# Separate banks for m and y, a shared ring for u and the transposes, u's products before the values', and the decayed keys on GpSimd

## The chip, the cores and the metric

The kernel runs on one core of one Trainium2 chip. The metric is the device time of one execution in microseconds. Five engines work side by side, each through its own queue in order: TensorE (PE, with its weight loads PEld), VectorE (DVE), ScalarE (ACT), GpSimd (POOL) and SyncE (SP, which here issues DMAs). Operands lie in SBUF; matmuls write to PSUM, which has 8 banks of 2 KB per partition.

## The reference

A linear attention with a decayed state feeds two expert layers. The change touches the attention alone.

```python
# B, H, S, D = 4, 8, 768, 48
for t in range(S):
    kt, vt, rt = (k[:, :, t], v[:, :, t], r[:, :, t])
    cur = np.einsum('bhd,bhe->bhde', u[None] * kt, vt)
    y[:, :, t] = np.einsum('bhd,bhde->bhe', rt, state + cur)
    state = w[None, :, :, None] * state + np.einsum('bhd,bhe->bhde', kt, vt)
# x = y as 3072 tokens x 384
expert_idx = np.argmax(xn @ en.T / tau, axis=1)      # xn, en: rows scaled to length 1
for e in range(8):                                   # one expert per token
    h = np.maximum(x[mask] @ w1[e], 0.0)
    out[mask] = gate_w[mask, None] * (h @ w2[e])
h = out @ w_in                                       # second layer, all tokens
y = (h * np.clip(h + 3.0, 0.0, 6.0) / 6.0) @ w_out
```

## The kernel before

The sequence is cut into 6 chunks of 128 tokens and the 8 heads into 4 pairs, so the attention has 24 groups (chunk c, head pair hp), each with all 4 batches. Within a chunk the recurrence becomes matmuls. For each group `load` (L556) brings four tiles from HBM through SP's queue: rk_t (r and k by dimension), tk (k by token), vd and vt (v by dimension and by token). rk_t and tk have three buffers, vd and vt five.

`scaled` (L656) multiplies r and k with powers of the decay: k_s (L659) and r_s (L660) on VectorE, rk_p (r times k, L662) on GpSimd, and kk, the keys by token times ktab (L666), on VectorE. kk is not made in the last chunk. `scores` (L669) makes the products of k_s and r_s on TensorE (L676); ScalarE copies them out (a_m, L679), and GpSimd sets the upper part to zero with two affine selects (L680). `current` (L685) makes m on TensorE (L691) from rk_p and the bonus u, and VectorE multiplies it with vd into mv (L693).

`outputs` (L696) makes y on TensorE: from the second chunk on the state's products (L704), then the values' products with the scores (L710), both into y_all; then u_ps (L717), the products of kk and vt for the next state. VectorE adds mv to y (y_sb, L719) and updates the state from u_ps (L724; in the first chunk ScalarE copies it, L722). `by_token` (L727) transposes y_sb on TensorE (L732) into x_ps, and ScalarE copies it into x_t (L735).

m and y are two halves of one tile, `my` of the pool psY (L653): for each of its two banks o, m has one half and y the other. u_ps has a bank of its own (psU), x_ps too (psX); psA holds two banks of scores, and psM has two buffers, which the routing's tiles (lt_ps, l_ps, rc_ps, li_ps), the tables' and the gathered rows' transposes (tp) take in turn. Together these are the 8 banks.

The loop over the groups (L765) does, for group i: the loads of group i+4; scores and m of group i+1; the transposes of group i-1; `scaled` for group i+2; in the first three groups of a chunk a step of the routing of the chunk before (`route`, L233); and the outputs of group i. TensorE's instructions keep this order (`pin`); on the other engines a planner orders them by their place in the program and by when it expects them to be ready. The routing sums a token's products with the expert directions, takes the best expert, its rank and weight, with some 20 short VectorE instructions per chunk (L253 to L303). It ends with the DMA that writes x_t to HBM (L306). x_t has two buffers; a memset on GpSimd (L758) opens each new one. From group 16 on, the first expert's weights are split on ScalarE and VectorE (`prep_w`, L203 and L206), and rows of the first expert are gathered and transposed. After the attention come the experts, and then the second layer.

Of the kernel before, what the change touches and what calls it, by code (L numbers as in the profile page):

```python
# [8 lines left out]
F32 = mybir.dt.float32  # L9
# [6 lines left out]
ALU = mybir.AluOpType  # L16
AX = mybir.AxisListType
ET = mybir.EngineType
PSUM = bass.MemoryType.PSUM
DRAM = bass.MemoryType.DRAM  # L20

B, H, S, D = 4, 8, 768, 48
# [4 lines left out]
C = 128  # L27
NCH = S // C
# [17 lines left out]
def rwkv_moe_kernel(ctx, tc, dT, tokA, wuT, uw, emb, tau, w1, w2, win, wout, out):  # L46
    nc = tc.nc
# [8 lines left out]
    psM = pctx.enter_context(tc.tile_pool(name="psM", bufs=2, space=PSUM))  # L56
# [56 lines left out]
    start = const.tile([128, E], F32, name="start")  # L113
# [429 lines left out]
    with actx:  # L543
# [6 lines left out]
        pa = ExitStack()  # L550
        psA = pa.enter_context(tc.tile_pool(name="psA", bufs=2, space=PSUM))
        psY = pa.enter_context(tc.tile_pool(name="psY", bufs=1, space=PSUM))
        psU = pa.enter_context(tc.tile_pool(name="psU", bufs=1, space=PSUM))
        psX = pa.enter_context(tc.tile_pool(name="psX", bufs=1, space=PSUM))

        def load(c, hp):  # L556
            rk_t = ld.tile([112, 2, B, C], F32, name="rk_t", tag="rk", bufs=3)
# [28 lines left out]
        ktab = st_p.tile([128, HP, 96], F32, name="ktab")  # L586
# [7 lines left out]
        n = 1  # L594
        while n < C:
            nc.vector.tensor_tensor(out=ptab[:, :, n + 1:2 * n + 1], in0=ptab[:, :, 1:n + 1],
                                    in1=ptab[:, :, n:n + 1].to_broadcast([112, HP, n]), op=ALU.mult)
# [52 lines left out]

        pin = tc.keep_in_program_order
        halves = ((0, 64), (64, 48))
        my = psY.tile([112, 2, 2, 2, C], F32, name="my")  # L653
        m_all, y_all = my[:, :, 0], my[:, :, 1]

        def scaled(c, hp, rk_t, tk, vd, vt):  # L656
            r_s = rk.tile([112, B, C], F32, name="r_s", tag="r", bufs=3)
            k_s = rk.tile([112, B, C], F32, name="k_s", tag="k")
            loads["k_s"] = nc.vector.tensor_tensor(out=k_s, in0=rk_t[:, 1], in1=itab[:, hp:hp + 1, :].to_broadcast([112, B, C]), op=ALU.mult).ins  # L659
            nc.vector.tensor_tensor(out=r_s, in0=rk_t[:, 0], in1=ptab[:, hp:hp + 1, 0:C].to_broadcast([112, B, C]), op=ALU.mult)  # L660
            rk_p = rk.tile([112, B, C], F32, name="rk_p", tag="ku")
            nc.gpsimd.tensor_tensor(out=rk_p, in0=rk_t[:, 0], in1=rk_t[:, 1], op=ALU.mult)  # L662
            kk = None
            if c < NCH - 1:
                kk = rk.tile([128, B, 96], F32, name="kk", tag="kk", bufs=3)
                nc.vector.tensor_tensor(out=kk, in0=tk, in1=ktab[:, hp:hp + 1, :].to_broadcast([128, B, 96]), op=ALU.mult)  # L666
            return r_s, k_s, rk_p, kk

        def scores(r_s, k_s):  # L669
# [14 lines left out]

        def current(c, hp, vd, rk_p):  # L685

            for o in range(2):
                for h in range(2):
                    q0, n = halves[(h + o) % 2]
                    r0 = 64 * h  # L690
                    pin(nc.tensor.matmul(m_all[q0:q0 + n, o], lhsT=ub[r0:r0 + 48, hp, 0:n], rhs=rk_p[r0:r0 + 48, 2 * o:2 * o + 2], start=True, stop=True))  # L691
            mv = rk.tile([112, B, C], F32, name="mv", tag="mv")
            nc.vector.tensor_tensor(out=mv.rearrange("p (o i) t -> p o i t", o=2), in0=m_all, in1=vd.rearrange("p (o i) t -> p o i t", o=2), op=ALU.mult)  # L693
            return mv

        def outputs(c, hp, vt, r_s, a_sb, kk, mv):  # L696
            s_n, s_o = (state[hp][(c - i) % 2] for i in range(2))
            if c > 0:
                for i in range(2):
                    for o in range(2):  # L700
                        for h in range(2):
                            q0, n = halves[(h + o) % 2]
                            r0, b = 64 * h, 2 * o + i
                            pin(nc.tensor.matmul(y_all[q0:q0 + n, o, i, :], lhsT=s_o[r0:r0 + 48, b, 0:n], rhs=r_s[r0:r0 + 48, b, :],  # L704
                                                 start=(i == 0), stop=False, skip_group_check=True))
            for o in range(2):
                for i in range(2):
                    for q, (q0, n) in enumerate(halves):
                        b = 2 * o + i
                        pin(nc.tensor.matmul(y_all[q0:q0 + n, o, i, :], lhsT=vt[:, b, q0:q0 + n], rhs=a_sb[(q + o) % 2][:, b, :],  # L710
                                             start=(c == 0), stop=True, skip_group_check=True))
            if c < NCH - 1:
                u_ps = psU.tile([112, B, D], F32, name="u_ps", tag="u")
                for b in range(B):
                    for h, (p0, n) in enumerate(halves):
                        v0 = 64 * ((h + b // 2) % 2)
                        pin(nc.tensor.matmul(u_ps[p0:p0 + n, b, :], lhsT=kk[:, b, 48 * h:48 * h + n], rhs=vt[:, b, v0:v0 + 48], start=True, stop=True))  # L717
            y_s = yp.tile([112, B, C], F32, name="y_sb", tag="y")
            loads["y_s"] = nc.vector.tensor_tensor(out=y_s.rearrange("p (o i) t -> p o i t", o=2), in0=y_all, in1=mv.rearrange("p (o i) t -> p o i t", o=2), op=ALU.add).ins  # L719
            if c < NCH - 1:  # L720
                if c == 0:
                    nc.scalar.copy(s_n[:, :, 0:D], u_ps)  # L722
                else:
                    nc.vector.scalar_tensor_tensor(out=s_n[:, :, 0:D], in0=s_o[:, :, 0:D], scalar=ptab[:, hp, C:C + 1], in1=u_ps, op0=ALU.mult, op1=ALU.add)  # L724
            return y_s

        def by_token(c, hp, x_t, y_s):  # L727

            x_ps = psX.tile([128, 2, 4, 64], F32, name="x_ps", tag="x")
            for b in range(B):  # L730
                o, i = divmod(b, 2)
                pin(nc.tensor.transpose(x_ps[:, i].rearrange("p s d -> p (s d)")[:, o * 128:o * 128 + 112], y_s[:, b, :], ident[0:112, 0:112]))  # L732
            for h, slots in enumerate((slice(0, 4, 3), slice(1, 3))):
                d0 = hp * 96 + h * D
                loads["x_t"] = nc.scalar.copy(out=x_t[:, :, d0:d0 + D].rearrange("p (o i) d -> p i o d", o=2), in_=x_ps[:, :, slots, 0:D]).ins  # L735
# [4 lines left out]
        def prepare(i):  # L740
            if i < len(groups):
                if i < HP:
                    tables(i)
                pre[i] = scaled(*groups[i], *data[i])

        def begin(i):
            if i < len(groups):
                r_s, k_s, rk_p, kk = pre[i]
                a_sbs[i] = scores(r_s, k_s)
                mvs[i] = current(*groups[i], data[i][2], rk_p)  # L750

        def moved(i):

            if i >= 0:
                c, hp = groups[i]
                if hp == 0:
                    xs[c] = xp.tile([128, B, DG], F32, name="x_t", tag="x", bufs=2)
                    nc.gpsimd.memset(xs[c][:, :, DM + 1:DG], 0.0)  # L758
                by_token(c, hp, xs[c], ys[i])
# [5 lines left out]
        for i, (c, hp) in enumerate(groups):  # L765
# [7 lines left out]
            if pend and hp < 3:  # L773
                rest += step(pend, 1) or []
            r_s, _, _, kk = pre.pop(i)
            ys[i] = outputs(c, hp, data[i][3], r_s, a_sbs.pop(i), kk, mvs.pop(i))
            if pend and hp == 3:
                step(pend, 1)
# [71 lines left out]
    with ExitStack() as mctx:  # L850
# [78 lines left out]
        for e in range(E):  # L929
# [35 lines left out]
            n = CAPS[e] if e else NL  # L965
# [322 lines left out]
```

## Time and profile before

| | us |
|---|---|
| median of 3 runs | 827.93 |
| lowest, highest | 824.88, 828.96 |
| the profiled execution | 831.06 |
| its span | 829.4 |

The profile shows one execution. Its times are microseconds from the start of the span unless marked ns. Lines such as L710 are lines of the kernel. The granted clock of TensorE is given as a share of full speed, where 1.00 is 2.4 GHz and 0.50 is 1.2 GHz. In a timeline, instructions of one line that follow each other are merged (x16); the idle time of the engine ahead of them and what ended it stand in brackets. Whom a wait is put down to is inferred from semaphores, and a wait for several of them is put down to the last.

| engine | busy us | share of the span |
|---|---|---|
| PE | 780.8 | 94% |
| DVE | 505.0 | 61% |
| ACT | 333.9 | 40% |
| POOL | 196.3 | 24% |

### The profile page before, as it was taken

The page shows a single profiled execution, that of the slowest core. Times are in us where ns is not written, and L with a number is a line of the kernel's source. Part 1 is how long each engine was busy: PE and PEld are TensorE (multiplying, and loading weights), DVE is VectorE, ACT ScalarE, POOL GpSimd, SP SyncE. Part 2 cuts the span into 40 slices and gives each one's busy share as a digit, 9 for nine tenths or more (in the row PEclk, how much of TensorE's full clock was granted, in tenths as well). Part 3 has the DMA queues.
Part 4 walks back from the last instruction along what each step waited for, and adds up shares of the span by engine and source line. Part 5 has one row for each costly group of instructions (what it writes and reads, how often), then busy time and mean ns, then how long its engine had stood idle before and what let it go on. Part 6 is the DMA issues. An engine that isn't in the chain of part 4 may idle for free. (4 is left out here: it accounts for less than half of the span.)

```text
span 829.4 us, 13926 instructions
## 1 busy us (share of the span) xinstructions
PE 780.8 (94%) x5353; PEld 698.8 (84%) x5354; DVE 505.0 (61%) x1031; ACT 333.9 (40%) x669; POOL 196.3 (24%) x222
## 2 busy tenths in 40 slices
PE   6879877899999999999989999999999999999995
PEld 3767655578999999998979898999998998999995
DVE  8585888864767778778468888453333343333331
ACT  3333424634455455546343434343333333333331
POOL 6543533613442242222202111210002002001001
PEclk8896998989999999999999999999999999999998
DMA  9865768315664666553312222010001001001001
GB/s 259 239 196 158 230 208 256 117 40 181 215 206 153 202 201 191 191 190 115 111 32 73 58 57 58 31 46 1 0 1 39 1 1 38 1 1 39 1 1 38
DMA packets 32235, 86.56 MB, mean 104 GB/s; under 512 B 4348, under 2 KB 15681, under 8 KB 32160
## 3 DMA queue, kind: packets, MB, share of 16 engines
q1 hardware_dynamic: 28480, 75.58, 29.6%
q0 software_dynamic: 3680, 10.01, 3.5%
q8 instruction: 44, 0.72, 0.4%
q14 instruction: 31, 0.25, 0.1%
HBM read 72.94 MB, written 12.63 MB: 103 GB/s over the span
## 5 line engine op out<-in xcount | busy, mean ns | idle before, releaser
L422 PE MATMUL l<-xh,whi 128*128 128x512 f32 (+9 forms) x504 | 184.5, 371 | 2.7 <-DVEq L1134 2.7
L423 PE MATMUL l<-xl,whi 128*128 128x512 f32 (+9 forms) x504 | 186.9, 372 | 0.0
L424 PE MATMUL l<-xh,wlo 128*128 128x512 f32 (+9 forms) x504 | 185.8, 369 | 0.0
L458 DVE SCALAR_TENSOR_TENSOR rg<-rg,l 128x512 f32<-128x512 f32 x96 | 65.7, 687 | 134.2 <-ACT rg L457 133.6
L457 ACT ACTIVATE rg<-l,nums 128x512 f32<-128x512 f32 x96 | 65.9, 689 | 172.8 <-PE l L424 160.3
L473 PE MATMUL o<-wlo,hh 128*128 128x384 f32 x384 | 128.9, 336 | 0.0
L472 PE MATMUL o<-whi,hh 128*128 128x384 f32 x384 | 128.1, 336 | 0.0
L474 PE MATMUL o<-whi,hl 128*128 128x384 f32 x384 | 124.4, 336 | 0.0
L422 PEld LDWEIGHTS l<-xh,whi 128*128 128x128 f32 x504 | 95.2, 190 | 13.8 <-issue 3.9
L424 PEld LDWEIGHTS l<-xh,wlo 128*128 128x128 f32 x504 | 95.7, 190 | 12.8
L423 PEld LDWEIGHTS l<-xl,whi 128*128 128x128 f32 x504 | 95.7, 190 | 10.1
L460 DVE TENSOR_TENSOR hl<-rg,hh 128x512 fp32r<-128x512 f32 x96 | 66.7, 696 | 48.6 <-ACT hh L459 45.2
L459 ACT CAST hh<-rg 128x512 fp32r<-128x512 f32 x96 | 59.4, 621 | 64.8 <-DVE rg L458 52.5
L1196 POOL DMA_INDIRECT out_dram<-o_t,ctok x20 | 20.8, 1040 | 255.4 <-ACT o_t L1194 252.1
L472 PEld LDWEIGHTS o<-whi,hh 128*128 128x128 f32 x384 | 72.4, 189 | 4.1
L473 PEld LDWEIGHTS o<-wlo,hh 128*128 128x128 f32 x384 | 72.5, 189 | 3.5
L523 DVE SCALAR_TENSOR_TENSOR hl<-l,hh 128x192 fp32r<-128x192 f32 (+8 forms) x72 | 37.5, 534 | 58.6 <-ACT hh L522 58.6
L474 PEld LDWEIGHTS o<-whi,hl 128*128 128x128 f32 x384 | 72.1, 189 | 0.2
L423 PE MATMUL acc<-hl,whi 128*128 128x192 f32 (+8 forms) x216 | 72.0, 335 | 0.2 <-DVE hl L523 0.2
L424 PE MATMUL acc<-hh,wlo 128*128 128x192 f32 (+8 forms) x216 | 72.1, 335 | 0.0
L522 ACT ACTIVATE hh<-l 128x192 fp32r<-128x192 f32 (+8 forms) x72 | 33.1, 474 | 85.3 <-PE l L424 79.9
L422 PE MATMUL acc<-hh,whi 128*128 128x192 f32 (+8 forms) x216 | 65.1, 335 | 0.6 <-DVE x L973 0.6
(221 smaller groups left out, 1151.4 us busy)
## 6 DMA issues: line engine op xcount, KB each, us to landing
wst<-in_w_dram SPq DMA_DIRECT2D x32, 768.0 KB
rk_t<-in_dT_dram SPq DMA_DIRECT2D x24, 448.0 KB
vd<-in_dT_dram SPq DMA_DIRECT2D x24, 224.0 KB
vt<-in_tok_dram SPq DMA_DIRECT2D x24, 224.0 KB
xs_d<-x_t SPq DMA_DIRECT2D x6, 776.0 KB
tk<-in_tok_dram SPq DMA_DIRECT2D x24, 192.0 KB
q<-in_win_dram SPq DMA_DIRECT2D x12, 384.0 KB
q<-in_wout_dram SPq DMA_DIRECT2D x12, 384.0 KB
```

The source lines that it names most:

```text
L422: pin(nc.tensor.matmul(ps, lhsT=w[0], rhs=x[0], start=first, stop=False))
L423: pin(nc.tensor.matmul(ps, lhsT=w[0], rhs=x[1], start=False, stop=False))
L424: pin(nc.tensor.matmul(ps, lhsT=w[1], rhs=x[0], start=False, stop=last))
L457: nc.scalar.activation(out=r6, in_=ps, func=AF.Relu, bias=three)
L458: nc.vector.scalar_tensor_tensor(out=gf, in0=r6, scalar=6.0, in1=ps, op0=ALU.min, op1=ALU.mult)
L459: nc.scalar.copy(out=gh, in_=gf)
L460: nc.vector.tensor_tensor(out=gl, in0=gf, in1=gh.bitcast(F32), op=ALU.subtract)
L472: pin(nc.tensor.matmul(acc[t], lhsT=gh[:, sl], rhs=wh[:, f % 4, :], start=(f == span[0]), stop=False))
L473: pin(nc.tensor.matmul(acc[t], lhsT=gh[:, sl], rhs=wl[:, f % 4, :], start=False, stop=False))
L474: pin(nc.tensor.matmul(acc[t], lhsT=gl[:, sl], rhs=wh[:, f % 4, :], start=False, stop=(f == span[1] - 1)))
L522: last["a"] = nc.scalar.activation(out=hh[:, 0:n], in_=ps[:, 0:n], func=AF.Relu).ins
L523: last["v"] = nc.vector.scalar_tensor_tensor(out=hl[:, 0:n], in0=ps[:, 0:n], scalar=0.0, in1=hh[:, 0:n].bitcast(F32), op0=ALU.max, op1=ALU ...
```

## The change

m and y get tiles of their own, each with two banks of which half is used; u_ps and x_ps no longer have pools of their own but take turns with the routing's tiles in psM, which keeps its two buffers. On TensorE u's products now stand between the state's products and the values'. kk is computed on GpSimd. Nothing else differs.

```diff
-        psU = pa.enter_context(tc.tile_pool(name="psU", bufs=1, space=PSUM))
-        psX = pa.enter_context(tc.tile_pool(name="psX", bufs=1, space=PSUM))
...
-        my = psY.tile([112, 2, 2, 2, C], F32, name="my")
-        m_all, y_all = my[:, :, 0], my[:, :, 1]
...
-                nc.vector.tensor_tensor(out=kk, in0=tk, in1=ktab[:, hp:hp + 1, :].to_broadcast([128, B, 96]), op=ALU.mult)
+                nc.gpsimd.tensor_tensor(out=kk, in0=tk, in1=ktab[:, hp:hp + 1, :].to_broadcast([128, B, 96]), op=ALU.mult)
...
         def current(c, hp, vd, rk_p):
 
+            m_all = psY.tile([112, 2, 4, C], F32, name="m_ps", tag="m")[:, :, 0:2]
...
         def outputs(c, hp, vt, r_s, a_sb, kk, mv):
             s_n, s_o = (state[hp][(c - i) % 2] for i in range(2))
+            y_all = psY.tile([112, 2, 4, C], F32, name="y_ps", tag="y")[:, :, 0:2]
...
+            if c < NCH - 1:
+                u_ps = psM.tile([112, B, D], F32, name="u_ps", tag="m")
+                for b in range(B):
+                    for h, (p0, n) in enumerate(halves):
+                        v0 = 64 * ((h + b // 2) % 2)
+                        pin(nc.tensor.matmul(u_ps[p0:p0 + n, b, :], lhsT=kk[:, b, 48 * h:48 * h + n], rhs=vt[:, b, v0:v0 + 48], start=True, stop=True))
             for o in range(2):
                 for i in range(2):
                     for q, (q0, n) in enumerate(halves):
                         b = 2 * o + i
                         pin(nc.tensor.matmul(y_all[q0:q0 + n, o, i, :], lhsT=vt[:, b, q0:q0 + n], rhs=a_sb[(q + o) % 2][:, b, :],
                                              start=(c == 0), stop=True, skip_group_check=True))
-            if c < NCH - 1:
-                u_ps = psU.tile([112, B, D], F32, name="u_ps", tag="u")
-                for b in range(B):
-                    for h, (p0, n) in enumerate(halves):
-                        v0 = 64 * ((h + b // 2) % 2)
-                        pin(nc.tensor.matmul(u_ps[p0:p0 + n, b, :], lhsT=kk[:, b, 48 * h:48 * h + n], rhs=vt[:, b, v0:v0 + 48], start=True, stop=True))
...
-            x_ps = psX.tile([128, 2, 4, 64], F32, name="x_ps", tag="x")
+            x_ps = psM.tile([128, 2, 4, 64], F32, name="x_ps", tag="m")
```

## Rows read from the trace of the kernel before

**Rows 1.** Windows: stretch, length, then busy us by engine, PE clock, DMA share, GB/s

```profile
60.00:70.00 10.00, 7.48 (x80) 5.94 (x79) 6.02 (x8) 1.78 (x6) 3.54 (x5) 0.61 0.72 201
70.00:80.00 10.00, 10.00 (x126) 7.06 (x124) 4.93 (x10) 5.32 (x16) 5.09 (x7) 0.70 0.40 115
...
200.00:250.00 50.00, 50.00 (x300) 46.63 (x299) 34.42 (x67) 26.37 (x54) 17.85 (x15) 1.00 0.59 194
```

**Rows 2.** Waits, 20 to 185 us: who for whom, us in total, times, longest

```profile
PE my L704 <- DVE mv L693: 14.1, 10, 4.3
...
PE my L691 <- DVE y_sb L719: 9.2, 6, 2.1
...
PE x_ps L732 <- DVE y_sb L719: 2.2, 2, 1.6
```

**Rows 3.** Timeline of PE: start us, us, line, operation, tiles, count, wait before

```profile
62.98 1.13 PE L704 MATMUL my<-r_s,state 48*64 48x128 f32 x16 [2.52 <-DVE mv L693]
...
84.28 0.66 PE L691 MATMUL my<-rk_p,ub 48*64 48x256 f32 x8 [2.00 <-DVE y_sb L719]
...
86.18 1.13 PE L704 MATMUL my<-r_s,state 48*64 48x128 f32 x16 [0.52 <-DVE mv L693]
...
100.08 1.16 PE L676 MATMUL a_ps<-r_s,k_s 48*128 48x128 f32 x16
...
104.81 1.16 PE L676 MATMUL a_ps<-r_s,k_s 48*128 48x128 f32 x16
...
118.30 0.67 PE L704 MATMUL my<-r_s,state 48*64 48x128 f32 x16 [2.37 <-DVE mv L693]
...
132.88 1.13 PE L704 MATMUL my<-r_s,state 48*64 48x128 f32 x16 [4.28 <-DVE mv L693]
...
138.66 0.60 PE L732 MATMUL x_ps<-ident,y_sb 112*128 112x112 f32 x4
...
145.97 0.67 PE L704 MATMUL my<-r_s,state 48*64 48x128 f32 x16 [1.44 <-DVE mv L693]
146.57 1.09 PE L710 MATMUL my<-a_m,vt 128*64 128x128 f32 x16
```

**Rows 4.** Timeline of DVE

```profile
59.41 2.91 DVE L659 TENSOR_TENSOR k_s<-rk_t,itab 112x512 f32<-112x512 f32 x1 [0.54 <-PE a_ps L676]
62.25 0.68 DVE L693 TENSOR_TENSOR mv<-my,vd 112x512 f32<-112x512 f32 x1
...
79.71 1.10 DVE L257 TENSOR_TENSOR lg<-lg,mx 128x32 f32<-128x32 f32 x1
...
83.48 0.66 DVE L719 TENSOR_TENSOR y_sb<-my,mv 112x512 f32<-112x512 f32 x1
...
128.26 3.96 DVE L659 TENSOR_TENSOR k_s<-rk_t,itab 112x512 f32<-112x512 f32 x1
...
136.15 0.66 DVE L719 TENSOR_TENSOR y_sb<-my,mv 112x512 f32<-112x512 f32 x1
```

**Rows 5.** Timeline of POOL

```profile
60.57 1.21 POOL L680 TENSOR_SCALAR_AFFINE_SELECT a_m<-a_m 128x512 f32<-128x512 f32 x2
61.76 1.70 POOL L662 TENSOR_TENSOR rk_p<-rk_t 112x512 f32<-112x512 f32 x1
...
79.49 1.27 POOL L662 TENSOR_TENSOR rk_p<-rk_t 112x512 f32<-112x512 f32 x1
89.40 0.11 POOL L758 MEMSET x_t<- 128x12 f32 x1 [8.64 <-DMA xs_d<-x_t]
...
144.91 1.49 POOL L680 TENSOR_SCALAR_AFFINE_SELECT a_m<-a_m 128x512 f32<-128x512 f32 x2
```

**Rows 6.** Single lines: ns min/median/max; for L666 the groups' busy us and mean ns

```profile
L659 DVE TENSOR_TENSOR k_s<-rk_t,itab x20: 676/692/3959, 25.2 to 150.6; 112x512 f32<-112x512 f32 x20
L693 DVE TENSOR_TENSOR mv<-my,vd x22: 673/683/693, 26.4 to 162.6; 112x512 f32<-112x512 f32 x22
L662 POOL TENSOR_TENSOR rk_p<-rk_t x21: 1251/1272/1811, 21.8 to 153.3; 112x512 f32<-112x512 f32 x21
...
L666 DVE TENSOR_TENSOR kk<-tk,ktab 128x384 f32<-128x384 f32 x20 | 12.6, 632 | 0.3 <-PE u_ps L717 0.2
```

## The prediction

> **What bounds the kernel now.** I read the windows first: they say which engine sets the pace of which part. From 200 to 250 us TensorE is busy in all of 50.00 us at clock 1.00 [rows 1], and the change touches nothing from there on. From 20 to 172 us, the attention with its 24 groups, it is different: in 60 to 70 us TensorE works 7.48 of 10 us, and at clock 0.61 [rows 1]. So the change is worth what it does to that stage, and what the stage gains reaches the end whole, because the experts' matmuls follow it on the same engine and wait for little else.
>
> The waits of that stage name the places [rows 2]. TensorE's y products wait for VectorE's mv (L704, 14.1 us in 10 waits), its m products for y_sb (L691, 9.2 us in 6), its transposes for y_sb (L732, 2.2 us in 2). The first two are waits for a shared bank: my keeps m and y of one half in one bank, so y may not be written while mv reads m, nor m while y_sb reads y. TensorE's order of time shows the single waits [rows 3], VectorE's and GpSimd's why they are long [rows 4, 5]. There are two kinds.
>
> In the first, k_s stands in front of mv on VectorE and doesn't get through. At 59.41 it took 2.91 us, where its median is 0.69; GpSimd ran one instruction after the other, and k_s ended 0.54 us after the affine selects did (62.32 against 61.78), while the rk_p behind them took 1.70, where its median is 1.27 [rows 4 to 6]. At 128.26 it took 3.96. So an instruction of VectorE with both inputs in SBUF waits for GpSimd, past several instructions. mv and y_sb, with one input in PSUM, don't: mv's longest is 693 ns [rows 6].
>
> In the second kind the routing's short instructions stand in front of y_sb. At 79.71 the subtraction L257, on 32 columns only, took 1.10, again to the end of a rk_p on GpSimd (79.49+1.27); y_sb began at 83.48 only, and m waited 2.00 [rows 3 to 5].
>
> **The change part by part.** All is against the profiled run's own 831.06 us (span 829.4); the median of the three runs, 827.93, lies 3.13 lower.
>
> Own banks, first kind. The waits of y for mv at 62.98, 118.30 and 132.88 are 2.52+2.37+4.28 = 9.17 [rows 3]. With y in its own banks TensorE goes on with y, u, values and the next scores. What is late next is m of the next group, which may not overwrite m before mv has read it, and the transposes, which need y_sb. At 132.88 the worst case is that k_s still ends at 132.22: then y_sb still ends at 136.8 (136.15 and its 0.66), and the transposes behind it start there and not at 138.66 [rows 3, 4]; gain 1.8 of 4.28. At the two others I take off one kk, 1.0, that lengthens GpSimd's run: 1.5+1.4. Together **-4.7** (0 to -9.2).
>
> Own banks, second kind. Three times a chunk's routing makes m wait about 2.0, and y behind it another 0.52 (one of the three at 84.28 and 86.18) [rows 3]. The 0.52 goes. The first wait moves to the transposes, which stand behind m; TensorE gains the 0.6 that m takes (0.66, less some overlap). But kk now follows rk_p on GpSimd and holds up the routing's two-input instructions: +1.0. Three times (-0.52-0.6+1.0) = **-0.4**. The three other waits of m (9.2 less 6.1) lose 0.6 each: **-1.8**.
>
> The rest of y's waits, 14.1-9.17-1.56 = 3.4, goes too, except at 145.97: the values behind it start at 146.57, and their affine select ended at 146.40 (144.91+1.49) [rows 3, 5]. Of its 1.44 only 0.2 is won: **-2.1**.
>
> The clock. After the wait at 62.98 it was 0.61 and then 0.70 in the windows to 80 us [rows 1], so 3.9+3.0 = 6.9 us at full clock were not granted, most of it under work. That fall goes only if the wait before it goes; I take half, **-2.5** (0 to -6.9). The falls behind the routing stay, since their waits stay about as long.
>
> kk on GpSimd. VectorE loses 20 instructions of 632 ns, 12.6 us [rows 6]. GpSimd has no such shape; its rk_p on 112x512 takes 1.25 to 1.27, so kk on 128x384 lies between 0.95 (by columns) and 1.27; 1.0, as it is the same operation with fewer columns. Five of the 20 are counted above. For the other 15: behind the values stand scores and m, about 1.7, before the transposes need y_sb, which takes 0.69, so a delay of 1.0 is just covered in the steady groups; it isn't where GpSimd catches up. That happens once a chunk: the memset of x_t held its queue for 8.64 us before 89.40 [rows 5], and affine, rk_p and now kk of two groups follow it without a break. I take 0.2 each, **+3.0** (0 to +15). On GpSimd's queue the affine selects stand behind kk; kk waits for u's products of three groups earlier, and those come before the scores that the next selects work on, so it holds none up for long. Also tk comes free on GpSimd now, and SP's loads queue behind it; kk is needed three groups later, so nothing.
>
> The Trainium skill, SBUF — State Buffer, section "Who interferes with whom", has a rule for this: a VectorE instruction with two SBUF inputs and a GpSimd instruction that reads SBUF exclude each other, and the second waits until the first has finished. The trace agrees that they exclude each other, but the 2.91 and 3.96 are longer than any GpSimd instruction beside them [rows 4, 5], so here one waits past several. By the rule alone the two long runs would not grow by kk, and the sum would be 2.0 better.
>
> Ring of two. u and x_ps share psM with the routing's four tiles. Without a routing tile between them each gets its own old slot back; with one they change places, and the transposes then wait for the state update that reads u, right behind the y_sb for which they wait anyway. The trace of before doesn't show these waits: 0 to +2, the width of a few y_sb and state updates on VectorE, because in one group the gathered rows' transposes come straight behind u; **+0.5**. u before the values gives the affine select 0.6 us more, and takes it from y_sb's lead over the next scores; both were counted.
>
> Sum: -4.7-0.4-1.8-2.1-2.5+3.0+0.5 = -8.0. Profiled 823.1; as a median **820**.
>
> **The rivals.** *A, the lock decides (slower).* GpSimd's run per group becomes 1.21+1.27+1.0 = 3.5 us, and VectorE's k_s and r_s, of one shape, need 1.4 between them: 4.9, more than the 4.73 us of a group without a wait (scores at 100.08 and 104.81) [rows 3, 5, 6]. From there every kk is on the path. In the sum, take out the 3.0 and the five of 1.0 and put in 20 of 1.0 to 1.27: -16.0+20 = +4 to +9, a median of 832 to 837. For it: VectorE is already late wherever TensorE waits. Against: VectorE gets 12.6 us back, and GpSimd idled 8.64 us in one go [rows 5], so its work isn't the limit, only its place. The Trainium skill, GPSIMD Engine Reference, section 4.1, speaks for A: two-input elementwise work belongs on VectorE, being about twice as slow on GpSimd. The trace agrees on the size: rk_p takes 1.27, k_s 0.69 on the same shape [rows 6].
>
> *B, the wait only moves.* y_sb sits in the same place on VectorE, and the transposes wait for it as y waited for mv. Then the 4.7 and the 2.5 are nothing: -0.8, a median of 827.
>
> *C, the waits go with their clock.* All of 9.17, no kk in the way (3×1.1, 1.8, 2.1), and 6.9 of clock: -23, a median of 805. Against it: the chain from the routing over the x_t write (8.64 us of waiting on GpSimd) to the affine select stays.
>
> **How the numbers follow.** About 0.5% (4 us) is what a measurement of this kernel can tell. Forecast 0.50, with its own range 813 to 826 by the bounds of the first-kind waits, of kk and of the ring; A 0.16, B 0.20, C 0.14. Faster by over 0.5%: C, nine tenths of the forecast and a little of B, 0.61; the same: most of B, the rest of the forecast and the low end of A, 0.24; slower 0.15. The range, leaving out a part of A above and of C below: 806 to 832.
>
> **What the profile after would show.** Right, if y's waits for mv are gone, if m waits for y_sb nowhere and the transposes do in the routing groups, about 2 us each, and if a k_s of 2 to 4 us still stands on VectorE without TensorE waiting beside it. kk should take about 1.0 on GpSimd. Wrong in A's way, if k_s, r_s and the routing's short instructions together take over 10 us more than now; in B's, if the transposes' waits reach some 20 us; and if u or the transposes wait for ScalarE or for the state, the ring was priced too low. What could make it all wrong is a planner that puts GpSimd's or VectorE's instructions in another order.

## The result

| | median us | lowest, highest | ratio to the kernel before (95%) |
|---|---|---|---|
| before | 826.98 | 824.88, 828.96 | |
| changed | 816.12 | 813.16, 820.24 | 0.9861 (0.9813 to 0.9909) |
| changed, measured again beside 828.35 | 812.10 | 808.53, 818.50 | 0.9818 (0.9766 to 0.9870) |

The change makes the kernel 1.4% faster, or 11 us; a second measurement says 1.8%, and the intervals overlap. The forecast was 820. In this document a median is over all executions of a kernel and a ratio over those that did not take clearly longer than the others; with u in y's banks (below), one of six took 1240 us, and the median of the other five is 812.91. The profiled execution of the changed kernel took 813.16 (span 811.5), 17.9 less than the profiled one of before. That pair overstates the gain, since one is the fastest run shown of its kernel and the other the slowest.

What the change touches ends where the first expert product starts on TensorE (L422): at 173.12 us before, at 160.98 after. So the attention gave 12.1 of the 17.9. The other 5.8 lies in work that is the same in both; in the kernels below that stretch, from the first expert product to the end of the run, took 652 to 659 us without any order, so I take it for chance.

Windows before and then after, the last one from 20 us to that product (columns: stretch, length, busy us of PE, PEld, DVE, ACT, POOL, PE clock, DMA share, GB/s):

```profile
50.00:60.00 10.00, 7.51 (x105) 6.10 (x104) 8.93 (x29) 2.42 (x7) 2.41 (x4) 0.83 0.60 192
...
130.00:140.00 10.00, 7.01 (x100) 5.97 (x100) 8.35 (x24) 2.01 (x6) 1.67 (x2) 0.66 1.03 298
...
20.00:173.12 153.12, 126.70 (x1835) 98.42 (x1835) 116.14 (x271) 61.97 (x167) 72.34 (x79) 0.86 0.64 192
```

```profile
50.00:60.00 10.00, 7.79 (x87) 6.25 (x88) 9.50 (x28) 2.70 (x7) 4.71 (x6) 0.64 0.82 252
60.00:70.00 10.00, 10.00 (x161) 7.60 (x161) 5.63 (x10) 4.99 (x15) 6.81 (x9) 0.85 0.63 171
70.00:80.00 10.00, 7.74 (x144) 5.92 (x143) 8.81 (x25) 3.25 (x9) 6.29 (x8) 1.00 0.69 211
...
130.00:140.00 10.00, 7.41 (x140) 5.85 (x140) 9.56 (x26) 6.32 (x15) 7.13 (x7) 1.00 0.51 163
...
20.00:160.98 140.98, 118.17 (x1816) 89.22 (x1812) 118.76 (x257) 60.14 (x165) 90.22 (x96) 0.91 0.75 213
```

TensorE has the same matmuls in both (1835 and 1816 of them in the records). Its idle time, length less busy time, went from 26.4 to 22.8; its busy time went from 126.70 to 118.17, at a granted clock of 0.91 in place of 0.86. So in this pair 3.6 of the 12.1 us are waits, and 8.5 are matmuls that took less time, at most 1.3 of it (19 of 1835) for records that are missing and the rest because more of them ran at 2.4 and not at 1.2 GHz. How it is shared out varies with the execution: in the profile of the changed kernel measured again (below) the waits fell by 9.8 and the matmuls by 7.1. Single windows show how the clock falls. [rows 1] had 0.61 and 0.70 at 60 to 80 us, behind the wait at 62.98; this wait is gone, and 0.85 and 1.00 stand there now. But at 50 to 60 us 0.83 became 0.64: a fall that lasts until about 63 us stands behind the two waits in a group with routing ("issue" means that the engine waited for nothing that the profile shows):

```profile
51.11 0.60 PE L730 MATMUL x_ps<-ident,y_sb 112*128 112x112 f32 x4 [1.16 <-DVE y_sb L717]
...
53.59 0.96 PE L709 MATMUL u_ps<-vt,kk 128*64 128x48 f32 x15 [1.10 <-issue]
...
56.32 2.08 PE L672 MATMUL a_ps<-r_s,k_s 48*128 48x128 f32 x16
```

Over 50 to 80 us what was not granted went from 1.7+3.9+3.0 = 8.6 to 3.6+1.5 = 5.1 us. At 130 to 140 us 0.66 became 1.00, but that is one execution: measured again, the changed kernel had 0.65 and 0.67 at 120 to 140 us. What its two profiles share is the sum: from 20 to 160 us 19.5 us were not granted before, and 12.9 and 13.9 after.

TensorE's waits after, 20 to 185 us (who for whom, us in total, times, longest), where [rows 2] had 14.1 for mv and 9.2 for y_sb:

```profile
PE x_ps L730 <- DVE y_sb L717: 15.8, 10, 3.1
PE u_ps L709 <- issue: 4.4, 4, 1.1
PE m_ps L688 <- DVE mv L690: 1.2, 2, 0.8
...
PE tp L404 <- DVE state L722: 0.7, 1, 0.7
PE u_ps L709 <- ACT x_t L733: 0.5, 1, 0.5
```

y waits for mv nowhere, and m for y_sb nowhere. What is left stands at the transposes, ten times, and at u, which had no wait before. TensorE's order of time shows both, against [rows 3]:

```profile
84.47 0.57 PE L730 MATMUL x_ps<-ident,y_sb 112*128 112x112 f32 x4 [1.98 <-DVE y_sb L717]
...
100.24 0.60 PE L730 MATMUL x_ps<-ident,y_sb 112*128 112x112 f32 x4 [1.16 <-DVE y_sb L717]
...
102.72 0.58 PE L709 MATMUL u_ps<-vt,kk 128*64 128x48 f32 x15 [1.09 <-issue]
...
104.17 1.16 PE L672 MATMUL a_ps<-r_s,k_s 48*128 48x128 f32 x16
...
109.06 0.98 PE L730 MATMUL x_ps<-ident,y_sb 112*128 112x112 f32 x4 [3.14 <-DVE y_sb L717]
```

VectorE after, for [rows 4]. The routing's subtraction L257 takes 2.06 where it took 1.10, the comparison L293 1.95 where it took 0.17, and r_s and k_s have runs of over 3 us still:

```profile
95.89 2.06 DVE L257 TENSOR_TENSOR lg<-lg,mx 128x32 f32<-128x32 f32 x1
...
103.16 1.95 DVE L293 TENSOR_TENSOR ge<-rank,row_f 128x12 f32<-128x12 f32 x1
...
118.91 3.62 DVE L656 TENSOR_TENSOR r_s<-rk_t,ptab 112x512 f32<-112x512 f32 x1 [2.21 <-PE u_ps L709]
...
123.37 3.03 DVE L655 TENSOR_TENSOR k_s<-rk_t,itab 112x512 f32<-112x512 f32 x1
```

GpSimd after, for [rows 5]:

```profile
79.40 1.26 POOL L658 TENSOR_TENSOR rk_p<-rk_t 112x512 f32<-112x512 f32 x1
80.63 0.99 POOL L662 TENSOR_TENSOR kk<-tk,ktab 128x384 f32<-128x384 f32 x1
84.05 0.11 POOL L756 MEMSET x_t<- 128x12 f32 x1 [2.43 <-DMA xs_d<-x_t]
...
96.90 1.00 POOL L662 TENSOR_TENSOR kk<-tk,ktab 128x384 f32<-128x384 f32 x1
...
104.08 1.00 POOL L662 TENSOR_TENSOR kk<-tk,ktab 128x384 f32<-128x384 f32 x1
```

kk takes 0.99. And the memset of x_t, which held GpSimd's queue for 8.64 us in [rows 5] and 38.8 us in four holds altogether, holds it for 2.43 here and 7.0 altogether. (A hold is the time that the queue stood still before the memset could start.) Nothing in the diff names it: in the changed kernel the planner queued the memset one group later, behind that group's selects, rk_p and kk.

### The profile page after: what moved, and what is told of

Its sections match the earlier page's. It is cut to its first block, busy times and chain, and to the rows that moved or that the text cites. A ratio compares the mean times of both kernels' runs of the same rounds, so it can differ in the third digit from the quotient of the medians.

```text
span 811.5 us, 13928 instructions
## 1 busy us (share of the span) xinstructions
PE 768.8 (95%) x5353; PEld 686.3 (85%) x5354; DVE 504.7 (62%) x1011; ACT 332.2 (41%) x669; POOL 213.9 (26%) x242
## 5 line engine op out<-in xcount | busy, mean ns | idle before, releaser
L422 PE MATMUL l<-xh,whi 128*128 128x512 f32 (+9 forms) x504 | 183.5, 369 | 1.7 <-DVEq L1132 1.7
L424 PEld LDWEIGHTS l<-xh,wlo 128*128 128x128 f32 x504 | 94.8, 188 | 12.9
L422 PEld LDWEIGHTS l<-xh,whi 128*128 128x128 f32 x504 | 94.4, 188 | 12.3 <-issue 2.5
L422 PE MATMUL acc<-hh,whi 128*128 128x192 f32 (+8 forms) x216 | 65.1, 334 | 0.6 <-DVE x L971 0.6
```

What stands on the lines that cost most here:

```text
L422: pin(nc.tensor.matmul(ps, lhsT=w[0], rhs=x[0], start=first, stop=False))
L424: pin(nc.tensor.matmul(ps, lhsT=w[1], rhs=x[0], start=False, stop=last))
```

## The experiments

Each is compared with runs of the kernel before on the same chip, whose medians were 828.55, 828.35 and 827.00 us in the three sets. The theories: **Banks**, the banks of m and y carry the gain. **Relief**, VectorE gains by losing kk. **Queue**, the new place of the memset in GpSimd's queue. **Ring**, the shared ring takes some 5 us back. **Lock**, VectorE's two-input instructions waiting for GpSimd. Busy and idle are TensorE's, from 20 us to the first expert product, read as above.

| kernel | median | ratio (95%) | busy | idle | clock |
|---|---|---|---|---|---|
| before | | 1 | 126.7 | 26.4 | 0.86 |
| changed | 816.12 | 0.9861 (0.9813 to 0.9909) | 118.2 | 22.8 | 0.91 |
| changed again | 812.10 | 0.9818 (0.9766 to 0.9870) | 119.6 | 16.6 | 0.90 |
| changed, kk on VectorE | 821.58 | 0.9930 (0.9894 to 0.9965) | 124.1 | 17.5 | 0.87 |
| the same, memset late | 814.24 | 0.9820 (0.9778 to 0.9863) | 121.2 | 17.5 | 0.89 |
| banks and ring alone | 820.07 | 0.9879 (0.9827 to 0.9931) | 124.5 | 19.1 | 0.88 |
| kk on GpSimd alone | 829.90 | 1.0015 (0.9979 to 1.0050) | 126.7 | 29.6 | 0.85 |
| memset late alone | 827.06 | 0.9958 (0.9920 to 0.9996) | 130.7 | 20.5 | 0.82 |
| ring alone | 824.86 | 0.9953 (0.9917 to 0.9989) | 129.7 | 24.0 | 0.83 |
| changed, u in y's banks | 814.04 | 0.9822 (0.9773 to 0.9871) | 119.6 | 16.2 | 0.89 |
| changed, u first | 824.26 | 0.9985 (0.9947 to 1.0022) | 134.1 | 16.1 | 0.84 |
| u first, kk on VectorE, memset late | 821.56 | 0.9942 (0.9911 to 0.9974) | 130.2 | 13.9 | 0.85 |
| changed, rk_p and kk on VectorE, memset late | 814.10 | 0.9834 (0.9786 to 0.9881) | 120.0 | 19.7 | 0.87 |
| changed, r_s on GpSimd too | 821.00 | 0.9935 (0.9913 to 0.9956) | 128.0 | 17.2 | 0.84 |

### One part at a time

kk alone, undone in the changed kernel and done in the one before, and the banks alone.

```diff
# changed, kk on VectorE
-                nc.gpsimd.tensor_tensor(out=kk, in0=tk, ...
+                nc.vector.tensor_tensor(out=kk, in0=tk, ...
```

> The changed kernel with kk back on VectorE; banks, ring and u's place stay as changed. Three theories are held against each other in these runs. Banks: the gain (10.9 us between the medians) comes from y's own banks, whose waits for mv are gone, and kk on GpSimd costs part of it back, since the routing's two-input instructions (L257 took 2.06, L293 1.92) wait behind it. Relief: the gain comes from VectorE being rid of kk (12.6 us). Queue: it comes from the planner, which now puts the memset of x_t (L758 of before) later in GpSimd's queue, so that it holds the queue for 1.3 to 2.4 us and not for 8.5 to 13. Banks expects 3 to 6 us less than the changed kernel, 810 to 813, with L257 near 1.1, L293 near 0.2 and the transposes' waits for y_sb (15.8) below 12. Relief expects 822 to 827. Queue expects a long hold of the memset and 820 to 827, as the planner has put it early again here, behind the rk_p of the group in which the routing's square roots are taken.

```diff
# the kernel before, kk on GpSimd
-                nc.vector.tensor_tensor(out=kk, in0=tk, ...
+                nc.gpsimd.tensor_tensor(out=kk, in0=tk, ...
```

> The kernel before with one edit: kk is computed on GpSimd. Banks, pools and TensorE's order stay as before. Banks expects no gain: y and m still wait in one bank, L257 and the others wait longer behind GpSimd, so 827 to 833. Relief expects most of the gain, 815 to 820. Queue expects a gain of some us if the memset's holds (8.5 to 13 us each before) shrink to 1 to 4, and none if they stay.

The third has kk on VectorE as well, and u's products behind the values again.

> The changed kernel with kk back on VectorE and u's products back behind the values': only the banks of m and y and the ring of two remain. Banks expects 808 to 814: y's waits for mv are gone, u's wait of 1.1 us for its slot in the ring (four times in the changed kernel) is covered by the values (1.05), and L257 takes about 1.1. If u's early place is what helps, this is slower than the run with only kk on VectorE by over 2 us. Relief expects 822 to 827. Queue expects a gain, as the planner puts the memset late here.

Measured: 821.58, 829.90 and 820.07. kk on GpSimd alone gives nothing, so Relief falls; the memset stayed early there, with 36.8 us of holds. Banks and ring alone give 1.2%, most of the change (here the planner happened to queue the memset later too; it held GpSimd for 13.1 us in all). But the changed kernel with kk on VectorE keeps only 0.7%, where Banks says that it should keep all. Its profile says what else came back with kk; GpSimd's and TensorE's waits in it:

```profile
POOL x_t L756 <- DMA xs_d<-x_t: 43.7, 4, 15.7
...
PE y_ps L714 <- POOL a_m L676: 6.1, 2, 4.5
```

The memset is early again, for 43.7 us, and now TensorE's values wait for the affine selects behind it. In the kernel before it was as early and the values waited 0.3 us in all, where TensorE had its waits for mv ahead of them [rows 2]:

```profile
PE my L710 <- POOL a_m L680: 0.3, 1, 0.3
```

### The memset's place

The memset queued behind the affine selects of the group begun in the same turn, in the kernel before and in the changed one with kk on VectorE.

```diff
-                nc.gpsimd.affine_select(out=a_m, ...)
+                loads["sel"] = nc.gpsimd.affine_select(out=a_m, ...).ins
...
-                    nc.gpsimd.memset(xs[c][:, :, DM + 1:DG], 0.0)
+                    behind(nc.gpsimd.memset(xs[c][:, :, DM + 1:DG], 0.0), "sel")
```

> The kernel before with one edit: the memset of x_t stands on GpSimd's queue behind the affine selects of the group that is begun in the same turn, so it comes some three groups later than the planner put it and should find x_t's old contents written. Queue expects the holds of 8.5 to 13 us (38 us in four) to fall below 2 each and most of the gain, 815 to 820. Banks expects little, 823 to 828: k_s still stands in front of mv, but GpSimd has shorter runs to catch up, so the three long waits of y for mv (9.2 us) may shrink to half.

> The changed kernel with the decayed keys back on VectorE, as in the run before, and with the memset of x_t queued behind the affine selects of the group that is begun in the same turn, so that it can't hold GpSimd in front of them. Queue (the loss of that earlier run, 821.58 against 816, was the memset's early place and not the keys): the values no longer wait for the affine selects (6.1 us in 2 there, 0 here), and the time is 814 to 818. Relief (VectorE needs to be rid of the keys): it stays at 820 to 823. If even less than 814, the keys are better off on VectorE.

> The changed kernel once more, unaltered, beside the others on the same chip. All theories: 814 to 819, a ratio of 0.984 to 0.990 to the kernel before.

Measured: 827.06 (ratio 0.9958) in the kernel before, 814.24 (0.9820) in the changed one with kk on VectorE, and 812.10 (0.9818) for the changed kernel beside it, where 814 to 819 was expected. Queue by itself, with its 815 to 820 in the kernel before, falls. With the memset late, kk's engine makes no difference that can be measured. With own banks the memset's place is worth 0.9930 against 0.9820, 1.1%; with shared banks it is worth 0.4%. Early, the banks (with the ring and u's place) gain only 0.7% (0.9930); late, 1.4% (0.9820 against 0.9958). That the place matters with own banks is clear of the noise; that the two help each other is likely, but at these intervals only just. The reading that fits: the banks let TensorE reach the values sooner, and a late memset lets the affine selects be ready when it does. What makes the planner choose isn't kk alone: with kk's engine alone undone the memset is early again (43.7 us of holds), but with kk on GpSimd alone it stayed early (36.8), and with banks and ring alone it came late with kk on VectorE (13.1).

### The ring

The ring alone in the kernel before, and the changed kernel with u out of the ring, in the unused half of y's banks.

```diff
# the kernel before
...
-                u_ps = psU.tile([112, B, D], F32, name="u_ps", tag="u")
+                u_ps = psM.tile([112, B, D], F32, name="u_ps", tag="m")
...
-            x_ps = psX.tile([128, 2, 4, 64], F32, name="x_ps", tag="x")
+            x_ps = psM.tile([128, 2, 4, 64], F32, name="x_ps", tag="m")
```

> The kernel before with one part of the change: u and the transposes take their turns in the routing's ring of two; m and y share their banks as before, u stands behind the values, the keys are on VectorE. The prediction's own step: plus 0.5 (0 to 2), 828 to 830 against 828.5. Ring (the ring costs about 5 us wherever it is): u waits four times about 1.1 us for a slot, and the time is 832 to 835. A third case: u behind the values comes 1.1 us later and finds its slot free, so the ring costs nothing here and something only with u in front of them: within 1 of the kernel before, no wait of u over 0.3.

```diff
# changed
-            y_all = psY.tile([112, 2, 4, C], F32, name="y_ps", tag="y")[:, :, 0:2]
+            y_ps = psY.tile([112, 2, 4, C], F32, name="y_ps", tag="y")
+            y_all, u_ps = y_ps[:, :, 0:2], y_ps[:, :, 2, 0:2 * D].rearrange("p o (i d) -> p o i d", i=2)
...
```

> The changed kernel, with u in the unused half of y's two banks instead of a turn of the ring; only the transposes and the routing still share it. The next y then waits for the state update that reads u, which runs on VectorE right behind y_sb. Ring: the four waits of u (4.4 us) and the one of the gathered rows' transposes for the state (0.7) are gone, and half to all of it reaches the end: 811 to 814. If the ring's waits only stand where the transposes would wait for y_sb anyway: the transposes' waits grow from 15.8 us by what u loses, and the time is the changed kernel's, 815 to 818.

Measured: 824.86 for the ring alone, a ratio of 0.9953, so it costs nothing there; it is even a little faster than any of the three expectations, and why is open. With u in y's banks 814.04, beside 812.10. TensorE's waits of the changed kernel measured again, and then with u in y's banks:

```profile
PE x_ps L730 <- DVE y_sb L717: 11.0, 10, 2.9
PE u_ps L709 <- issue: 3.3, 3, 1.1
PE u_ps L709 <- PE y_ps L702: 1.0, 1, 1.0
...
PE x_ps L730 <- ACT a_m L675: 0.7, 1, 0.7
```

```profile
PE x_ps L730 <- DVE y_sb L717: 14.7, 10, 2.8
```

u's waits are gone. The transposes wait 14.7 us for y_sb, between the 11.0 and the 15.8 of the changed kernel's two profiles, so that u's waits moved there isn't shown. But the time is that of the changed kernel beside it, whose ratio is 0.9818 where this one's is 0.9822: the ring's four waits of about 1.1 are real, and nothing of them reaches the end that can be measured. Ring, with its 5 us, falls.

### The order of u and the transposes

u's products moved ahead of the transposes, to give y_sb more time; once in the changed kernel as it is, once with kk on VectorE and the memset late.

```diff
             begin(i + 1)
+            u_now = update(c, hp, data[i][3], pre[i][3])
             moved(i - 1)
...
```

`update` holds u's products, which `outputs` made before.

> The changed kernel with one thing moved: u's products stand ahead of the transposes of the group before, and no longer between the state's products and the values'. Moved wait (what is left of the waits sits at the transposes, which come too early for y_sb): y_sb gains the 0.6 to 0.95 us that u takes, the ten waits of the transposes (11 to 16 us in all) fall by about 5, and the time is 807 to 812. If u's wait for a slot of the ring comes along and y_sb starts as late as before: 812 to 817, no change.

> The same move of u, with the decayed keys on VectorE and the memset of x_t queued behind the affine selects (that kernel without the move took 814.24). Moved wait: 808 to 812. If the keys' engine makes no difference, as the earlier pair says (814.24 and 812.10), it comes out within 3 us of the run beside it that only moves u.

Measured: 824.26 and 821.56. Nearly all of the gain is gone in the one, more than half in the other; the expectations ran from 807 to 817 and had it slower nowhere. TensorE's waits in the first, and its order of time:

```profile
PE x_ps L734 <- DVE y_sb L721: 6.3, 6, 1.8
PE r_ps L273 <- DVE state L726: 3.7, 4, 0.9
```

```profile
104.54 0.60 PE L734 MATMUL x_ps<-ident,y_sb 112*128 112x112 f32 x4 [1.21 <-DVE y_sb L721]
106.06 0.18 PE L273 MATMUL r_ps<-ohot,tri 128*128 128x32 bf16 x1 [0.92 <-DVE state L726]
...
106.33 1.13 PE L712 MATMUL y_ps<-r_s,state 48*64 48x128 f32 x16
107.40 1.97 PE L718 MATMUL y_ps<-a_m,vt 128*64 128x128 f32 x16
109.29 2.08 PE L672 MATMUL a_ps<-r_s,k_s 48*128 48x128 f32 x16
```

The transposes do wait less, 6.3 in place of 11.0, as meant. But u now takes its slot of the ring ahead of the routing's tiles, and these wait for the state update that reads it (8.4 us for r_ps in the second kernel). These waits come from the ring. Yet TensorE's idle time is no longer than in the changed kernel, 16.1 and 13.9 against 16.6. What grew is its busy time, 134.1 and 130.2 against 119.6, at clock 0.84 and 0.85. After the two waits above the scores took 2.08 us; they take 1.16 at full clock. The memset was early in the first (36.8 us of holds) and late in the second, so it can explain no more than the difference of the two. Why the clock fell more often with no more idle time is not settled. In the profile of the changed kernel the waits at 100.24 and 102.72 were followed by scores of 1.16; measured again, the same two waits (1.16 and 1.10) were followed by a fall:

```profile
96.33 0.60 PE L730 MATMUL x_ps<-ident,y_sb 112*128 112x112 f32 x4 [1.16 <-DVE y_sb L717]
...
98.81 0.78 PE L709 MATMUL u_ps<-vt,kk 128*64 128x48 f32 x15 [1.10 <-issue]
...
99.49 1.93 PE L714 MATMUL y_ps<-a_m,vt 128*64 128x128 f32 x15
101.35 1.67 PE L672 MATMUL a_ps<-r_s,k_s 48*128 48x128 f32 x16
```

### How much the lock is worth

GpSimd's products taken away, and one added.

```diff
# changed, kk on VectorE, memset late
-            nc.gpsimd.tensor_tensor(out=rk_p, in0=rk_t[:, 0], ...
+            nc.vector.tensor_tensor(out=rk_p, in0=rk_t[:, 0], ...
```

> The changed kernel with the keys and rk_p too on VectorE, the memset behind the affine selects: GpSimd is left with the affine selects and a few small instructions. Lock (k_s, r_s and the routing's subtractions are long because GpSimd's run of products holds them up): no k_s or r_s over 1.6 us is left, their means fall from about 1.1 us to 0.7 to 0.8. Whether that is worth anything: VectorE takes on some 24 times 0.7 = 17 us and loses some 15 us of waiting, so Banks says 811 to 817, no change; if the waiting were what the transposes wait for, 805 to 810; if VectorE's queue is the limit, above 820.

```diff
# changed
-            nc.vector.tensor_tensor(out=r_s, in0=rk_t[:, 0], ...
+            nc.gpsimd.tensor_tensor(out=r_s, in0=rk_t[:, 0], ...
```

> The changed kernel with one more product, r_s, moved to GpSimd, to find the point from which the lock decides. By rival A's own working GpSimd then has two selects (1.6), rk_p (1.4), kk (1.07) and r_s (about 1.35) per group: 5.4 us, against some 4.7 us of a group without a wait on TensorE, before any k_s is let in (0.7). So 0.7 to 1.4 us more in each of 20 to 24 groups: 826 to 846, and TensorE's m, scores or values wait for GpSimd in most groups. If the products give way to each other and only the order counts: within 5 of the changed kernel.

Measured: 814.10 and 821.00. r_s and k_s (VectorE's lines, 20 to 170 us: busy us, mean ns, then idle before) in the changed kernel measured again, and without rk_p and kk on GpSimd:

```profile
L656 DVE TENSOR_TENSOR r_s<-rk_t,ptab 112x512 f32<-112x512 f32 x21 | 25.3, 1203 | 5.6 <-PE y_ps L702 5.3 <-DMA rk_t<-in_dT_dram 0.2
L655 DVE TENSOR_TENSOR k_s<-rk_t,itab 112x512 f32<-112x512 f32 x21 | 23.1, 1100 | 2.7 <-PE a_ps L672 2.7
```

```profile
L655 DVE TENSOR_TENSOR k_s<-rk_t,itab 112x512 f32<-112x512 f32 x20 | 14.6, 730 | 8.4 <-PE a_ps L672 5.5 <-DMA rk_t<-in_dT_dram 2.2 <-DMA vd<-in_dT_dram 0.4
L656 DVE TENSOR_TENSOR r_s<-rk_t,ptab 112x512 f32<-112x512 f32 x20 | 13.9, 693 | 5.0 <-PE y_ps L702 3.3 <-DMA rk_t<-in_dT_dram 1.7
```

The long runs are GpSimd's doing: without rk_p and kk there the means fall from 1203 and 1100 to 693 and 730 ns, and L257 from 1265 to 232 (both of 6). The time stays. So in the changed kernel the lock takes some 18 us on k_s and r_s and 12 on L257 and L293 (7.1 and 1.0 us in all for L293), and VectorE has them to spare: in their place it did 16 us of rk_p and 10 of kk. With a third product on GpSimd the loss is about 1% (0.9935 against 0.9818 and 0.9861), not the 826 to 846 that rival A's working gives. Again most of it is clock: idle 17.2, busy 128.0, against 16.6 and 119.6. So that it is the lock which begins to decide there is likely, but not shown: the order of u and the transposes cost as much with no product moved.

## Why the prediction was right, and where not

**The size.** The attention's term was -8.0; the profile shows -12.1. Beside the medians, 820 was 4 and 8 us too long. The term that is furthest off is the clock's. The waits and kk and the ring together were put at -5.5 (-4.7-0.4-1.8-2.1+3.0+0.5), and TensorE's idle time fell by 3.6, in the second profile by 9.8; that is right in size, though with a price for kk that wasn't paid and a memset that the sum didn't have (below). The clock was put at -2.5, half of one fall, and TensorE's busy time fell by 8.5 and 7.1. The step that failed here is that it counted one fall alone, the one behind the wait at 62.98, halved it, and let the others stay. That fall went whole, its 6.9 us with its wait. The others changed too: the one behind the routing's waits grew from 1.7 to 5.1 us over 50 to 70 us, against "the falls behind the routing stay", and the rest of the 6.6 (19.5 less 12.9; 5.6 in the second profile) came from windows that were in no term, and not from the same ones in both profiles. Rival C was right on this one fall, which goes with its wait, and wrong on the waits; that its 6.9 is near the whole of the clock's gain is luck.

**Own banks, first and second kind.** As told: the waits for mv and for y_sb at m left TensorE's list, and the transposes wait in their place, at most 3.14 us. One thing was told wrong: "a k_s of 2 to 4 us without TensorE waiting beside it". The r_s of 3.62 us at 118.91 ends at 122.53, y_sb follows, and the transposes behind it waited 2.39 at 123.59; only the k_s after it had no wait beside it. B's reading, that all of it moves there, falls: 15.8 us stand at the transposes now, below B's 20, and the listed waits for mv and y_sb together went from 25.5 (14.1+9.2+2.2) to 17.0 (15.8+1.2).

**kk on GpSimd, +3.0.** The duration was right (1.0 told, 0.99), and so was what it does to L257 (+1.0 told, 1.10 to 2.06). Not seen was L293, from 0.17 to 1.95: at 103.16 it lasted until kk had ended on GpSimd (105.11 and 105.08), as L257 did a group and a half earlier with its own (97.95 and 97.90). The cost is nothing that can be measured (814.24 with kk on VectorE, 812.10 with kk on GpSimd), inside the bounds of 0 to 15 but at their lower end: 15 steady groups at 0.2 each was too dear, as the lock falls into VectorE's spare time. The Trainium skill, GPSIMD Engine Reference, section 4.1, speaks against the move, two-input elementwise work being about twice as slow there. The trace agrees on the direction, with 0.99 against 0.63 [rows 6], 1.6 times, and the runs show that this price need not be paid where neither engine is the limit.

**What kk did by another way.** The prediction named a planner that puts GpSimd's instructions in another order as what could make it all wrong. It did, and in the change's favour: the memset went behind the selects, worth 1.1% with own banks. By the prediction's own account of C, in which the chain from the routing over the x_t write to the affine select stays, the gain would have been near that of the changed kernel with kk on VectorE, 0.9930, some 6 us. That is less than the 8.0 of the sum, and the sum without its 3.0 for kk was 11.0. So part of the agreement is luck: a term that was not in the sum, and of the right sign, made up for what the waits gave less.

**The ring, +0.5.** Right in price; wrong in what would show it. "If u or the transposes wait for ScalarE or for the state, the ring was priced too low": u did wait, 4.4 us that the profile puts down to "issue" and 0.5 for ScalarE, and the price was nothing that can be measured. So a wait in the list is not yet a cost.

**Rival A.** Its 4.9 us per group, taken as a bound, never held the kernel: of 42 k_s and r_s of the changed kernel 8 took over 1.3 us, and 5 of these lie before 36 us. Yet the sign that was to tell A from the forecast did show: k_s, r_s, L257 and L293 took 25.1+19.0+4.2+1.0 = 49.3 us over the whole run before and 22.0+25.7+7.1+7.1 = 61.9 after, 12.6 more where "over 10" was to mean A, and the kernel was faster all the same. The sign was wrong and not the forecast: a longer time on VectorE counts only where TensorE waits for it.

## What to carry to other kernels

Where an engine stands still often and briefly, count two things from the windows, idle time and busy time at the granted clock: here the waits gave 3.6 us and the matmuls, of which fewer ran at 1.2 GHz, 8.5 us, and in a second profile 9.8 and 7.1. After any change read the order of every queue again, of instructions that the diff doesn't name too: a 0.11 us memset that waits for a DMA was worth 1.1% with own banks and 0.4% without. And don't price a wait by its place in the list alone: u's 4.4 us were taken out, and the time stayed.

## What the runs showed of the hardware

VectorE's instructions with both inputs in SBUF wait past several instructions of GpSimd: r_s took 3.62 us at 118.91, where it takes 0.68 undisturbed. Beside it stood, on the changed kernel's GpSimd, two affine selects, rk_p, kk and the beginning of a small product:

```profile
118.52 1.23 POOL L676 TENSOR_SCALAR_AFFINE_SELECT a_m<-a_m 128x512 f32<-128x512 f32 x2
119.72 1.26 POOL L658 TENSOR_TENSOR rk_p<-rk_t 112x512 f32<-112x512 f32 x1
120.94 0.99 POOL L662 TENSOR_TENSOR kk<-tk,ktab 128x384 f32<-128x384 f32 x1
121.89 1.54 POOL L223 TENSOR_TENSOR ny<-ss,nums 128x4 f32<-128x4 f32 x1
```

Without rk_p and kk on GpSimd none took over 1.13. The Trainium skill, SBUF — State Buffer, section "Who interferes with whom", has the one that comes second wait for the instruction that holds the shared ports; the rows agree on who excludes whom, not on one instruction being the limit. Even a subtraction on 128x32 elements, 0.23 us undisturbed, took 2.06.

Less idle time is not always a better clock. The kernel before with the memset late had 5.9 us less idle time than without (20.5 against 26.4) and 4.0 us more busy time (130.7 against 126.7), at a granted clock of 0.82 against 0.86. Busy and idle are of one profiled execution each, so a single difference of a few us there may be chance. Over the table it is not: the five kernels with a ratio below 0.987 have 118 to 121 us of busy time, the seven at 0.9935 and above 127 to 134, while idle time runs from 16 to 23 in the ones and 14 to 30 in the others.

Two things were not tried: m and y with one bank each, which would have left u and the transposes their own, and m and y as two tiles in the banks they shared. So it is shown that y's waits for mv go with separate tiles in separate banks, and argued that the bank, and not the common tile, made them.
